# Linear attention into a two-layer token network: the order of the last two token tiles, and the last 128 tokens in two pieces

## The chip, the cores and the metric

The kernel runs on one core of one Trainium2 chip. The core has a matrix engine (TensorE, "PE" in the profile, with "PEld" for its weight loads), VectorE ("DVE"), ScalarE ("ACT"), GpSimd ("POOL") and SyncE ("SP"), which here only issues DMA transfers. Each engine runs its own list of instructions in order and waits on semaphores for the others; a DMA is issued by an engine's queue and carried out by 16 DMA engines. Matmuls write to PSUM, whose banks hold 512 float32 columns of 128 partitions each; everything else lives in SBUF. The metric is the device time of one execution in microseconds; lower is better.

## The reference

```python
def _attn_ref(q, k, v):                    # 8 blocks x 8 heads x 576 positions x 64
    q_s = np.exp(q - np.max(q, axis=-1, keepdims=True))
    q_s = q_s / (np.sum(q_s, axis=-1, keepdims=True) + 1e-09)
    k_s = np.exp(k - np.max(k, axis=2, keepdims=True))
    k_s = k_s / (np.sum(k_s, axis=2, keepdims=True) + 1e-09)
    kv = np.einsum('bhsd,bhse->bhde', k_s, v)
    return np.einsum('bhsd,bhde->bhse', q_s, kv)

def _moe_ref(x, w_in, w_out):              # x: 4608 x 512, w_in: 512 x 2048, w_out: 2048 x 512
    h = x @ w_in
    g = np.maximum(0.01 * h, h)
    return g @ w_out
```

The attention's output, with its heads side by side, is `x`. Inputs and output are float32.

## The kernel before

**Tiles.** The 4608 tokens are nine tiles of 512 (`TT`), numbered 0 to 8; the attention has eight blocks `b` of 576 tokens, so block 7 covers tokens 4032 to 4607: the last 64 of tile 7 and all of tile 8. `xT` holds the attention's output in bf16, features on partitions. For tiles 1 to 6 the loop at L916 does layer 1 as 16 groups `j` of four matmuls (`layer1`, L564), each into a PSUM bank `ph` that ScalarE turns into half of a tile `gj` with a leaky ReLU (`leaky`, L573); then layer 2 as four groups `tsub` of 128 tokens and 16 matmuls each (`layer2`, L585) into a bank `pout`, copied to `out_sb` and stored by two DMAs of 64 rows (`store`, L577 to L582). `layer2_at` (L907) is a generator that yields after each matmul.

**Banks.** `psB` has six PSUM banks for nearly everything, `psO` two for `pout`. `out_sb` has four buffers, `gj` ten, the raw inputs six.

**Attention between the groups.** `at(t, u, ...)` hangs work on a place: `u` from 0 to 15 is after layer-1 group `u` of tile `t`, 16 to 31 after each quarter of its layer-2 groups. For a block these are: loads; `k_front` and `k_exp` (softmax over positions); `q_front` (maximum, L244, and subtraction, L303), `q_exp` (L311), `q_back` (sum, L320; reciprocal; normalization, L327; and `q_turn`, a transposing DMA by SyncE, L552); `attend_kv` (L505), which multiplies keys and values of the next block (`kv_quads`, L340) and queries with them (`cross`, L478), and `kd_make` (L360, L361). `x_keep` (L501 on ScalarE, L503 on VectorE) copies the result from `po` banks into `xT`. For the last block `attend_all` (L535) does queries alone, at place (6, 19), after tile 6's first layer-2 group; its 16 matmuls use six banks.

**The last two tiles as a pair.** Layer 1 of tiles 7 (`TA`, tokens `XA`) and 8 (`TB`, tokens `XB`) is one 2 x 2 block product (the two tiles by the two halves of the features `CL`, `CR`; these by the two halves of the hidden units), done with seven products in place of eight. `weight_sums` (L791, at place (6, 12)) makes the four combinations of weights `t1` to `t4` in VectorE (four subtractions of 2048 columns, L789) and a copy `b22` on GpSimd; `token_sums` (L801, at (6, 22)) makes `s1` to `s4` on VectorE (L810, L789) and `a22` on ScalarE (L813), all float32 for the matmuls. `pair_layer1(i, between)` (L951) does *block row* `i` of eight: seven `product`s of two matmuls each (L948), in this order: the first one from `xT` and `w_in` as they are, `p6` (`t2` by `s2`), `p2` (`xT` and `w_in`), `t3` by `s3`, `p5` (`t1` by `s1`), `t4` by `a22`, `b22` by `s4`. ScalarE copies the first to `e1` (L967), VectorE adds the others up in seven additions (`add`, L960), and ScalarE applies the leaky ReLU to four results: two for tile 7 (`g7`, in `gj` tiles; the fourth one of a row is held until the next row has begun, `held_leaky`), two for tile 8 (`g8`, in columns of `xT` whose tiles are done). After each product the generator `between_products` (L987) issues a *filler*, one layer-2 matmul (two after the seventh): in rows 0 and 1 tile 6's last group, from row 2 on the pair's own layer 2 for tile 7, `pair_layer2` (L937), four matmuls each on the activations of row `n - 2`. Its four banks are the two of `psO` and two of `psB`, so from row 2 on four banks are left for products. After the rows come the last 16 of these matmuls, four copies by VectorE and stores; then layer 2 of tile 8, four groups (L1018), each copied by ScalarE and stored.

Of the kernel before, what the change touches and what calls it, by code (L numbers as in the profile page):

```python
# [26 lines left out]
def kernel(  # L27
# [737 lines left out]
    for t in range(3, B - 1):  # L765
        b = t + 1
        q_front(b, t - 1, 29)
        at(t, 2, lambda b=b: q_exp(b, ALLR))
        if b + 1 < B:
            k_front(b + 1, t, 1, 8)  # L770
            casts(b + 1, t, 6)
            at(t, 17, lambda b=b: k_exp(b + 1, ALLH))
            at(t, 23, lambda b=b: attend_kv(b))
        q_back(b, t, 5)
        if b + 2 < B:
            at(t, 5, lambda b=b: load_all(b + 2))
# [38 lines left out]

    at(6, 12, weight_sums)
    at(6, 19, lambda: attend_all(B - 1, (R7,), (RE,)))
    at(6, 22, token_sums)

# [86 lines left out]

    def layer2_at(t, g, tsub, po):  # L907
        for j in range(NF):
            layer2(po, g, tsub, j)
            if j == NF - 1:  # L910
                store(t * TT + tsub * P, po, nc.scalar.copy)
            if j % 4 == 3:
                run(t, 16 + 4 * tsub + j // 4)
            yield

    for t in range(1, TA):  # L916
        g_sb = []
        for j in range(NF):
            ph = psB_pool.tile([P, TT], FP32, name="ph", tag=BANK_TAG)
            layer1(j, ph, t * TT, TT)  # L920
            if j % 2 == 0:
                g_sb.append(g_pool.tile([P, 2, TT], BF16, name="gj"))
            leaky(g_sb[j // 2][:, j % 2], ph)
            run(t, j)
        for tsub in range(NTS):
            po = psO_pool.tile([P, O], FP32, name="pout", tag="pout")
            fill = layer2_at(t, g_sb, tsub, po)
            if (t, tsub) != (TA - 1, NTS - 1):
                for _ in fill:
                    pass  # L930


    g7 = {}
    g8 = lambda j: xT[:, j % NB, j // NB * TT : (j // NB + 1) * TT]

    def pair_layer2(tsub, po, j):
        nc.tensor.matmul(  # L937
            po,
            lhsT=g7[j][:, tsub * P : (tsub + 1) * P],
            rhs=w_out_sb[:, j],  # L940
            start=(j == 0),
            stop=(j == NF - 1),
        )

    def product(i, w, a):
# [3 lines left out]
        return ps  # L949

    def pair_layer1(i, between):  # L951
        of = lambda n: (lambda c: late[n][:, c])
        wl = lambda c0: (lambda c: w_in_sb[:, c0 + c])
        xl = lambda c0: (lambda c: xT[:, c0 + c, XA])
        e1, u2, u3, u4, c22 = (late["pool"].tile([P, TT], FP32, name=n) for n in ("e1", "u2", "u3", "u4", "c22"))
        pair = g_pool.tile([P, 2, TT], BF16, name="gj")
        g7[i], g7[NH + i] = pair[:, 0], pair[:, 1]

# [7 lines left out]

        nc.scalar.copy(out=e1, in_=do(wl(0), xl(0)))  # L967
        for fn in held_leaky:
            fn()
        p6 = do(of("t2"), of("s2"))  # L970
        p2 = do(wl(2), xl(2))
        add(u2, p6, e1)
        add(e1, p2, e1)
        leaky(g7[i], e1)
        add(u3, do(of("t3"), of("s3")), u2)
        p5 = do(of("t1"), of("s1"))
        add(u4, p5, u2)
        add(c22, p5, u3)
        leaky(g8(NH + i), c22)
# [4 lines left out]

    pouts, held_leaky = [], []

    def between_products():  # L987
        for n in range(NH):
            if n < 2:
                todo = [lambda: next(fill, None)] * 8  # L990
            else:
                if n == 2:
                    pouts.extend(psO_pool.tile([P, O], FP32, name="pout", tag="pout") for _ in range(2))
                    pouts.extend(psB_pool.tile([P, O], FP32, name="pout2", tag=BANK_TAG) for _ in range(2))
                todo = [
                    lambda tsub=tsub, j=j: pair_layer2(tsub, pouts[tsub], j)
                    for j in (n - 2, NH + n - 2)
                    for tsub in range(NTS)
                ]
            for k in range(7):  # L1000
                for fn in todo[k : k + 1 + k // 6]:
                    fn()
                yield

    between = between_products()
    for i in range(NH):
        pair_layer1(i, between)
    held_leaky[0]()
    for i in range(NH - 2, NH):
        for j in (i, NH + i):  # L1010
            for tsub in range(NTS):
                pair_layer2(tsub, pouts[tsub], j)
    for tsub in range(NTS):
        store(TA * TT + tsub * P, pouts[tsub])
    for tsub in range(NTS):
        po = psB_pool.tile([P, O], FP32, name="pout2", tag=BANK_TAG)
        for j in range(NF):
            nc.tensor.matmul(  # L1018
                po,
                lhsT=g8(j)[:, tsub * P : (tsub + 1) * P],  # L1020
                rhs=w_out_sb[:, j],
                start=(j == 0),
                stop=(j == NF - 1),
            )
        store(TB * TT + tsub * P, po, nc.scalar.copy)
    assert not hooks, list(hooks)
# [30 lines left out]
```

## Time and profile before

| | |
|---|---|
| time, median of 3 runs | 282.3 us (282.1 to 282.39) |
| the profiled execution | 282.17 us |
| its span in the profile | 280.4 us |
| its mean granted TensorE clock | 0.997 |
| TensorE busy | 270.9 us, 97% of the span |
| VectorE busy | 208.8 us, 74% |
| ScalarE busy | 164.4 us, 59% |
| GpSimd busy | 50.4 us, 18% |
| end of tile 6's layer 1 | 205.82 us |
| the eight block rows | 216.90 to 257.90 us |
| start of tile 8's layer 2 | 261.77 us |

The span is what the profiler saw, from the first instruction to the last event; the rest of the execution's time lies around it. In a timeline a line gives start and duration in microseconds, the engine, the line of the kernel, the operation, `out<-in` and the shape; brackets behind it give the idle time before it and what ended that. The chain of waits is followed back from the last instruction, and tells which engine set the end at each moment. A view by stretches cuts the span at given times, with each engine's busy time and number of instructions in each stretch.

### The profile page before, as it was taken

The numbers are of one execution on the slowest core, as the hardware profiler recorded it, in microseconds if no ns is written. First come the engines' busy times: TensorE is split into PE (matmuls) and PEld (weight loads), VectorE is DVE, ScalarE is ACT, GpSimd is POOL, SyncE is SP. The second block draws the span as 40 slices with busy tenths as digits, with TensorE's granted clock in tenths as the row PEclk, the third lists the DMA queues.
The fourth block names the chain that finished last, engine by engine and source line by source line (L and its number), as shares of the span: only waits on it lengthen the run. The fifth ranks groups of instructions, "written<-read, shape, count | busy, mean of one in ns | idle before, by whom it ended". The sixth has DMA issues, their size and how long they took to land.

```text
span 280.4 us, 4875 instructions
## 1 busy us (share of the span) xinstructions
PE 270.9 (97%) x1895; PEld 134.3 (48%) x1922; DVE 208.8 (74%) x292; ACT 164.4 (59%) x291; POOL 50.4 (18%) x56
## 2 busy tenths in 40 slices
PE   8899999999999999999999999999999989999993
PEld 3488644444444554445444444444444545544441
DVE  3986986999999959948793779452898788888400
ACT  4977483782597368744775467644845555655220
POOL 2957460358003004000400050100000000000000
PEclk9999999999999999999999999999999999999998
DMA  7999999986992697099219830333033110000273
GB/s 254 327 207 325 250 233 310 394 292 177 351 408 87 101 385 258 8 320 353 65 32 315 315 79 2 84 77 75 1 87 75 37 37 2 0 1 0 65 162 75
DMA packets 39847, 46.46 MB, mean 166 GB/s; under 512 B 18704, under 2 KB 23056, under 8 KB 39824
## 3 DMA queue, kind: packets, MB, share of 16 engines
q1 hardware_dynamic: 36320, 41.95, 47.8%
q0 software_dynamic: 3504, 4.20, 8.6%
q8 instruction: 15, 0.25, 0.3%
q14 instruction: 8, 0.07, 0.1%
HBM read 36.70 MB, written 9.44 MB: 165 GB/s over the span
## 4 chain that ended last, share of the span: by engine, by line
PE 83%; DVE 9%; ACT 2%; issue 2%; DMA 2%; SPq 0%; DVEq 0%
PE pout L585 35%; PE ph L564 34%; PE pout L1018 5%; DVE u L960 4%; PE pp L948 4%; DMA k_raw<-in_k_dram 2%; PE po L478 2%; PE pout L937 1%; DVE e L960 1%; DVE c L960 1%; DVE t L159 1%; PE pokv L340 1%; ACT e L967 1%; PE pkv L340 1%; PE pkv L418 0%
## 5 line engine op out<-in xcount | busy, mean ns | idle before, releaser
L585 PE MATMUL pout<-w_out_sb,gj 128*128 128x512 bf16 x432 | 100.6, 379 | 1.1 <-issue 0.3
L564 PE MATMUL ph<-xT,w_in_sb 128*128 128x512 bf16 (+1 forms) x505 | 98.3, 352 | 0.4
L573 ACT ACTIVATE gj<-ph 128x512 bf16<-128x512 f32 x112 | 63.2, 603 | 17.6 <-PE ph L564 16.7
L564 PEld LDWEIGHTS <-w_in_sb 128*128 128x128 bf16 x512 | 49.8, 98 | 47.0 <-DMA w_in_sb<-in_moe_w_in_dram 0.3
L585 PEld LDWEIGHTS <-gj 128*128 128x128 bf16 x448 | 42.8, 98 | 52.4 <-issue 2.9
L579 ACT COPY out_sb<-pout 128x512 f32<-128x512 f32 x28 | 16.3, 583 | 52.7 <-PE pout L585 19.4
L217 POOL CAST vb<-v_raw 128x1152 bf16<-128x1152 f32 x13 | 20.1, 1577 | 83.7 <-DMA v_raw<-in_v_dram 67.8
L320 DVE TENSOR_REDUCE qsum<-qe 128x36 f32<-128x2304 bf16 (+5 forms) x13 | 20.1, 1542 | 10.5 <-ACT qe L311 10.3
L205 ACT ACTIVATE ke<-k_raw 128x2304 bf16<-128x2304 f32 (+2 forms) x13 | 18.0, 1386 | 9.4 <-DVE k_raw L197 9.0
L327 DVE TENSOR_TENSOR qe<-qe,qrec 128x2304 bf16<-128x2304 bf16 (+5 forms) x13 | 21.5, 1657 | 0.4
L960 DVE TENSOR_TENSOR u<-pp,u 128x512 f32<-128x512 f32 x32 | 20.6, 684 | 0.8
L937 PE MATMUL pout<-w_out_sb,gj 128*128 128x512 bf16 x62 | 20.4, 384 | 0.7 <-ACT out_sb L579 0.6
L244 DVE TENSOR_REDUCE qmax<-q_raw 128x36 f32<-128x2304 f32 (+5 forms) x13 | 20.0, 1540 | 0.3 <-DMA q_raw<-in_q_dram 0.3
L311 ACT ACTIVATE qe<-q_raw 128x2304 bf16<-128x2304 f32 (+5 forms) x13 | 17.1, 1317 | 4.4 <-POOL q_raw L303 3.5
L197 DVE TENSOR_TENSOR k_raw<-k_raw,kall 128x1152 f32<-128x1152 f32 (+2 forms) x10 | 18.1, 1821 | 0.3
L948 PE MATMUL pp<-s,t 128*128 128x512 f32 x48 | 18.2, 479 | 0.0
L360 DVE RECIPROCAL krec<-pokv 128x2 f32<-128x2 f32 x8 | 1.3, 165 | 20.4 <-PE pokv L478 20.4
L303 POOL TENSOR_TENSOR q_raw<-q_raw,qmax 128x512 f32<-128x512 f32 (+3 forms) x7 | 11.8, 1682 | 20.7 <-DVE qmax L244 20.2
L501 ACT CAST xT<-po 128x448 bf16<-128x448 f32 (+3 forms) x34 | 14.4, 516 | 1.1 <-PE po L478 1.1
L159 DVE TENSOR_TENSOR t<-t 128x256 f32<-128x256 f32 (+2 forms) x22 | 14.0, 637 | 0.7
L1018 PE MATMUL pout<-w_out_sb,xT 128*128 128x512 bf16 x62 | 13.9, 379 | 0.1
L303 DVE TENSOR_TENSOR q_raw<-q_raw,qmax 128x2304 f32<-128x2304 f32 (+1 forms) x6 | 13.2, 2202 | 0.2
(97 smaller groups left out, 247.5 us busy)
## 6 DMA issues: line engine op xcount, KB each, us to landing
out_dram<-out_sb SPq DMA_DIRECT2D x72, 128.0 KB, 3.0
q_raw<-in_q_dram SPq DMA_DIRECT2D x6, 1152.0 KB, 9.2
v_raw<-in_v_dram SPq DMA_DIRECT2D x6, 1152.0 KB, 11.9
k_raw<-in_k_dram SPq DMA_DIRECT2D x5, 1152.0 KB, 6.6
k_raw<-in_k_dram SPq DMA_DIRECT2D x6, 576.0 KB, 6.1
v_raw<-in_v_dram SPq DMA_DIRECT2D x4, 576.0 KB, 7.5
w_in_sb<-in_moe_w_in_dram POOLq DMA_DIRECT2D x7, 256.0 KB, 7.1
w_out_sb<-in_moe_w_out_dram POOLq DMA_DIRECT2D x6, 256.0 KB, 9.5
```

Of the source, the lines that this page charges most:

```text
L217: eng.tensor_copy(out=o, in_=i)
L244: nc.vector.tensor_reduce(out=o, in_=st[b]["q"][:, hs, rs], axis=AX.X, op=ALU.max)
L303: eng.tensor_tensor(out=qs, in0=qs, in1=st[b]["qmax", rs.start, hs.start].unsqueeze(3).to_broadcast([P, m, n, D]), op=ALU.subtract,)
L320: nc.vector.reduce_sum(out=qsum, in_=q_cols(b, rs, hs), axis=AX.X)
L327: nc.vector.tensor_tensor(out=qes if out is None else out, in0=qes, in1=st[b]["qrec", rs.start, hs.start].unsqueeze(3).to_broadcast([P, n, ...
L564: nc.tensor.matmul(ph, lhsT=w_in_sb[:, cb, j * P : (j + 1) * P], rhs=xT[:, cb, c0 : c0 + n], start=(cb == 0 and first), stop=(cb == NB - 1 ...
L573: nc.scalar.activation(out=o, in_=ph, func=AF.Prelu, alpha=LEAKY_SLOPE)
L585: nc.tensor.matmul(pout, lhsT=g_sb[j // 2][:, j % 2, tsub * P : (tsub + 1) * P], rhs=w_out_sb[:, j, os], start=(j == 0), stop=(j == NF - 1),)
L937: nc.tensor.matmul(po, lhsT=g7[j][:, tsub * P : (tsub + 1) * P], rhs=w_out_sb[:, j], start=(j == 0), stop=(j == NF - 1),)
L948: nc.tensor.matmul(ps, lhsT=w(c)[:, i * P : (i + 1) * P], rhs=a(c), start=(c == 0), stop=(c == 1))
L960: nc.vector.tensor_tensor(out=o, in0=ps, in1=e, op=ALU.add)
L1018: nc.tensor.matmul(po, lhsT=g8(j)[:, tsub * P : (tsub + 1) * P], rhs=w_out_sb[:, j], start=(j == 0), stop=(j == NF - 1),)
```

## The change

*Block 7's queries* (hunk 1): `q_front(7)` goes to (5, 19), `q_exp(7)` to (5, 24), `q_back(7)` to (5, 25); before, these stood at (5, 29), (6, 2) and (6, 5). *The head of the pair* (hunk 2): `weight_sums` goes to (6, 2); the last `attend_all` and `token_sums` to (6, 15), that is between tile 6's two layers, with `x_keep` shared out to ScalarE and VectorE. *Tile 6's layer 2*: only its first group comes ahead of the pair; the other three are the fillers of rows 0 to 5. *First products*: `pair_first(i + 1)` issues the first product of a row and its copy to `e1` in row `i`, between `p5` and `t4`. `g7` of rows 2 to 7 goes to columns of `xT` that are done. *The pair's layer 2*: in row 6 `pair_step` does four matmuls each for groups 2 and 3 (banks of `psB`), in row 7 four each for groups 0 and 1 (banks of `psO`); 48 more follow the rows. *Tile 8's layer 2*: the first three groups are copied by VectorE; the last one is done as 384 and then 128 columns, copied by ScalarE and VectorE, with one of the two DMAs of each issued by ScalarE.

```diff
@@ -763,15 +763,15 @@
     at(2, 22, lambda: k_exp(4, H0), lambda: k_exp(4, H1))
     at(2, 27, lambda: attend_kv(3))
     for t in range(3, B - 1):
-        b = t + 1
-        q_front(b, t - 1, 29)
-        at(t, 2, lambda b=b: q_exp(b, ALLR))
-        if b + 1 < B:
+        b, last = t + 1, t + 2 == B
+        q_front(b, t - 1, 19 if last else 29)
+        at(t - last, 24 if last else 2, lambda b=b: q_exp(b, ALLR))
+        if not last:
             k_front(b + 1, t, 1, 8)
             casts(b + 1, t, 6)
             at(t, 17, lambda b=b: k_exp(b + 1, ALLH))
             at(t, 23, lambda b=b: attend_kv(b))
-        q_back(b, t, 5)
+        q_back(b, t - last, 25 if last else 5)
         if b + 2 < B:
             at(t, 5, lambda b=b: load_all(b + 2))
 
@@ -813,9 +813,8 @@
         nc.scalar.copy(out=late["a22"], in_=xT[:, CR, XB])
         subtract(nc.vector, "s4", xT[:, CR, XA], plain("s2"))
 
-    at(6, 12, weight_sums)
-    at(6, 19, lambda: attend_all(B - 1, (R7,), (RE,)))
-    at(6, 22, token_sums)
+    at(6, 2, weight_sums)
+    at(6, 15, lambda: attend_all(B - 1, (R7, (nc.scalar, nc.vector)), (RE, (nc.scalar, nc.vector))), token_sums)
 
     def g_tiles():
         return [g_pool.tile([P, 2, TT], BF16, name="gj") for _ in range(NF // 2)]
@@ -904,7 +903,8 @@
     for tsub in range(NTS):
         store(tsub * P, pout[tsub])
 
-    def layer2_at(t, g, tsub, po):
+    def layer2_at(t, g, tsub):
+        po = psO_pool.tile([P, O], FP32, name="pout", tag="pout")
         for j in range(NF):
             layer2(po, g, tsub, j)
             if j == NF - 1:
@@ -922,25 +922,14 @@
                 g_sb.append(g_pool.tile([P, 2, TT], BF16, name="gj"))
             leaky(g_sb[j // 2][:, j % 2], ph)
             run(t, j)
-        for tsub in range(NTS):
-            po = psO_pool.tile([P, O], FP32, name="pout", tag="pout")
-            fill = layer2_at(t, g_sb, tsub, po)
-            if (t, tsub) != (TA - 1, NTS - 1):
-                for _ in fill:
-                    pass
+        for tsub in range(NTS if t < TA - 1 else 1):
+            for _ in layer2_at(t, g_sb, tsub):
+                pass
 
 
     g7 = {}
-    g8 = lambda j: xT[:, j % NB, j // NB * TT : (j // NB + 1) * TT]
-
-    def pair_layer2(tsub, po, j):
-        nc.tensor.matmul(
-            po,
-            lhsT=g7[j][:, tsub * P : (tsub + 1) * P],
-            rhs=w_out_sb[:, j],
-            start=(j == 0),
-            stop=(j == NF - 1),
-        )
+    spent = lambda n: xT[:, n % NB, n // NB * TT : (n // NB + 1) * TT]
+    g8 = spent
 
     def product(i, w, a):
         ps = psB_pool.tile([P, TT], FP32, name="pp", tag=BANK_TAG)
@@ -948,13 +937,22 @@
             nc.tensor.matmul(ps, lhsT=w(c)[:, i * P : (i + 1) * P], rhs=a(c), start=(c == 0), stop=(c == 1))
         return ps
 
+    of = lambda n: (lambda c: late[n][:, c])
+    firsts, held_leaky = {}, []
+
+    def pair_first(i):
+        firsts[i] = e1 = late["pool"].tile([P, TT], FP32, name="e1")
+        ps = product(i, lambda c: w_in_sb[:, c], lambda c: xT[:, c, XA])
+        nc.scalar.copy(out=e1, in_=ps)
+
     def pair_layer1(i, between):
-        of = lambda n: (lambda c: late[n][:, c])
-        wl = lambda c0: (lambda c: w_in_sb[:, c0 + c])
-        xl = lambda c0: (lambda c: xT[:, c0 + c, XA])
-        e1, u2, u3, u4, c22 = (late["pool"].tile([P, TT], FP32, name=n) for n in ("e1", "u2", "u3", "u4", "c22"))
-        pair = g_pool.tile([P, 2, TT], BF16, name="gj")
-        g7[i], g7[NH + i] = pair[:, 0], pair[:, 1]
+        e1 = firsts[i]
+        u2, u3, u4, c22 = (late["pool"].tile([P, TT], FP32, name=n) for n in ("u2", "u3", "u4", "c22"))
+        if i < 2:
+            pair = g_pool.tile([P, 2, TT], BF16, name="gj")
+            g7[i], g7[NH + i] = pair[:, 0], pair[:, 1]
+        else:
+            g7[i], g7[NH + i] = (spent(NF + 2 * (i - 2) + n) for n in range(2))
 
         def add(o, ps, e):
             nc.vector.tensor_tensor(out=o, in0=ps, in1=e, op=ALU.add)
@@ -964,17 +962,17 @@
             next(between)
             return ps
 
-        nc.scalar.copy(out=e1, in_=do(wl(0), xl(0)))
+        add(u2, do(of("t2"), of("s2")), e1)
         for fn in held_leaky:
             fn()
-        p6 = do(of("t2"), of("s2"))
-        p2 = do(wl(2), xl(2))
-        add(u2, p6, e1)
-        add(e1, p2, e1)
+        add(e1, do(lambda c: w_in_sb[:, 2 + c], lambda c: xT[:, 2 + c, XA]), e1)
         leaky(g7[i], e1)
         add(u3, do(of("t3"), of("s3")), u2)
         p5 = do(of("t1"), of("s1"))
         add(u4, p5, u2)
+        if i + 1 < NH:
+            pair_first(i + 1)
+            next(between)
         add(c22, p5, u3)
         leaky(g8(NH + i), c22)
         add(u3, do(of("t4"), of("a22")), u3)
@@ -982,47 +980,67 @@
         add(u4, do(of("b22"), of("s4")), u4)
         held_leaky[:] = [lambda: leaky(g7[NH + i], u4)]
 
-    pouts, held_leaky = [], []
+    pouts, started = {}, [0] * NTS
+    turn = [j for i in range(NH) for j in (i, NH + i)]
+
+    def pair_step(tsub):
+        j = turn[started[tsub]]
+        started[tsub] += 1
+        if tsub not in pouts:
+            pool, tag = (psO_pool, "pout") if tsub < 2 else (psB_pool, BANK_TAG)
+            pouts[tsub] = pool.tile([P, O], FP32, name="pout", tag=tag)
+        nc.tensor.matmul(
+            pouts[tsub],
+            lhsT=g7[j][:, tsub * P : (tsub + 1) * P],
+            rhs=w_out_sb[:, j],
+            start=(started[tsub] == 1),
+            stop=(started[tsub] == NF),
+        )
+
+    def fill_steps():
+        for tsub in range(1, NTS):
+            yield from layer2_at(TA - 1, g_sb, tsub)
+        for tsubs in ((2, 3), (0, 1)):
+            for _ in range(4):
+                for tsub in tsubs:
+                    pair_step(tsub)
+                    yield
 
     def between_products():
+        fill = fill_steps()
         for n in range(NH):
-            if n < 2:
-                todo = [lambda: next(fill, None)] * 8
-            else:
-                if n == 2:
-                    pouts.extend(psO_pool.tile([P, O], FP32, name="pout", tag="pout") for _ in range(2))
-                    pouts.extend(psB_pool.tile([P, O], FP32, name="pout2", tag=BANK_TAG) for _ in range(2))
-                todo = [
-                    lambda tsub=tsub, j=j: pair_layer2(tsub, pouts[tsub], j)
-                    for j in (n - 2, NH + n - 2)
-                    for tsub in range(NTS)
-                ]
             for k in range(7):
-                for fn in todo[k : k + 1 + k // 6]:
-                    fn()
+                for _ in range(1 + k // 6):
+                    next(fill)
                 yield
 
     between = between_products()
+    pair_first(0)
+    next(between)
     for i in range(NH):
         pair_layer1(i, between)
     held_leaky[0]()
-    for i in range(NH - 2, NH):
-        for j in (i, NH + i):
-            for tsub in range(NTS):
-                pair_layer2(tsub, pouts[tsub], j)
+    next(between, None)
+    while started[0] < NF:
+        for tsub in range(NTS):
+            pair_step(tsub)
     for tsub in range(NTS):
         store(TA * TT + tsub * P, pouts[tsub])
     for tsub in range(NTS):
-        po = psB_pool.tile([P, O], FP32, name="pout2", tag=BANK_TAG)
-        for j in range(NF):
-            nc.tensor.matmul(
-                po,
-                lhsT=g8(j)[:, tsub * P : (tsub + 1) * P],
-                rhs=w_out_sb[:, j],
-                start=(j == 0),
-                stop=(j == NF - 1),
-            )
-        store(TB * TT + tsub * P, po, nc.scalar.copy)
+        row0 = TB * TT + tsub * P
+        last = tsub == NTS - 1
+        pieces = ((slice(0, 384), nc.scalar.copy), (slice(384, O), nc.vector.tensor_copy))
+        for os, copy in pieces if last else ((slice(0, O), nc.vector.tensor_copy),):
+            po = psB_pool.tile([P, os.stop - os.start], FP32, name="pout2", tag=BANK_TAG)
+            for j in range(NF):
+                nc.tensor.matmul(
+                    po,
+                    lhsT=g8(j)[:, tsub * P : (tsub + 1) * P],
+                    rhs=w_out_sb[:, j, os],
+                    start=(j == 0),
+                    stop=(j == NF - 1),
+                )
+            store(row0, po, copy, os, (nc.sync, nc.scalar) if last else (nc.sync, nc.sync))
     assert not hooks, list(hooks)
```

## The prediction

> **What bounds the kernel now.** I read the page's first two parts, then the chain of waits, then stretches cut at the borders of the last stages, then the timelines of TensorE, VectorE and ScalarE there, and last the stores at the end.
>
> ```profile
> span 280.4 us, 4875 instructions
> PE 270.9 (97%) x1895; PEld 134.3 (48%) x1922; DVE 208.8 (74%) x292; ACT 164.4 (59%) x291; POOL 50.4 (18%) x56
> PE 83%; DVE 9%; ACT 2%; issue 2%; DMA 2%; SPq 0%; DVEq 0%
> ...
> 205.82 1.08 PE pout L585 x5
> 209.28 0.61 PE po L478 x16
> 209.89 5.07 PE pout L585 x23
> ```
>
> TensorE sets the end nearly everywhere; only its gaps and what follows its last matmul can be won. From the end of tile 6's first layer (205.82) one layer-2 group of 16 matmuls takes 209.28 - 205.82 = 3.46 us, the last attention 0.61. DVE's 9% of the chain lies in the paired rows, so those are cut out next, one row to a stretch (columns: length, busy time of PE, PEld, DVE, ACT, POOL, clock, DMA):
>
> ```profile
> 216.90:221.88 4.98, 4.98 (x24) 2.67 (x22) 3.71 (x7) 2.16 (x4) 0.00 (x0) 1.00 0.23 53
> ...
> 226.86:232.62 5.76, 5.12 (x24) 2.74 (x22) 4.49 (x8) 3.41 (x7) 0.00 (x0) 1.00 0.20 46
> ...
> 252.80:257.90 5.10, 5.10 (x23) 2.42 (x21) 4.32 (x7) 2.90 (x5) 0.00 (x0) 1.00 0.00 0
> ```
>
> In the timeline of TensorE stands what stopped row 2, and in the chain how the rows end:
>
> ```profile
> 228.62 0.38 PE L937 MATMUL pout<-w_out_sb,gj 128*128 128x512 bf16 x1 [0.64 <-ACT out_sb L579]
> 260.73 1.04 PE pout L937 x4
> 261.77 0.22 PE pout L1018
> 272.83 2.77 PE pout L1018 x12
> ```
>
> Row 0 runs at 4.98 us, busy throughout: TensorE's own pace for 7 products and 8 layer-2 matmuls. Row 2 takes 5.76: its first matmul into a `pout` bank of its own waits 0.64 us for ScalarE to empty tile 6's. The eight rows end at 257.90, so they take 41.00 us where 8 x 4.98 = 39.84 would do: 1.16 lost. (PE looks full in the last row, at 5.10, because a matmul that waits for its operands counts as busy.) The 16 matmuls from 257.90 to 261.77 take 3.87 against 3.46: 0.41 more, spent on the last activation of row 7. Together 1.57 us.
>
> The timelines of VectorE and ScalarE over one of the late rows:
>
> ```profile
> 239.59 0.69 DVE L960 TENSOR_TENSOR u<-pp,e 128x512 f32<-128x512 f32 x1 [0.57 <-ACT e L967]
> ...
> 242.97 1.29 DVE L960 TENSOR_TENSOR u<-pp,u 128x512 f32<-128x512 f32 x2
> 244.84 0.69 DVE L960 TENSOR_TENSOR u<-pp,e 128x512 f32<-128x512 f32 x1 [0.57 <-ACT e L967]
> ...
> 243.70 0.63 ACT L573 ACTIVATE xT<-u 128x512 bf16<-128x512 f32 x1 [0.16 <-DVE u L960]
> 244.24 0.57 ACT L967 COPY e<-pp 128x512 f32<-128x512 f32 x1
> ```
>
> This is the loop of the late rows. VectorE's seven additions run from 239.59 to 242.97 + 1.29 = 244.26; then it idles for 0.57 us until ScalarE has copied the next row's first product (244.24 to 244.81), which stands behind an activation in ScalarE's order. Period: 244.84 - 239.59 = 5.25 us, against TensorE's 4.98. Without the idle time VectorE needs some 4.67 a row.
>
> **The change, part by part.** *First product ahead.* It takes its bank and its copy into `e1` before the last three additions of the row before. The copy then waits only for its product and for the activation of `e1`, both done by mid row. VectorE's period falls to 4.67 and TensorE's 4.98 leads; 0.31 us a row is there to catch up. The number of products and fillers stays 56 and 64.
>
> *Tile 6's layer 2 as filler.* Three of its groups (48 matmuls) move into rows 0 to 5; rows 6 and 7 start the pair's layer 2 on activations of rows 0 and 1, long done; the other 48 follow the rows. The 0.64 us goes, since no `pout` bank is wanted just after a group's end, and the last activation is wanted some 40 matmuls (9 us) after row 7, so the 0.41 goes. In rows 0 to 5 all six banks serve products. In rows 6 and 7 four do, as before in rows 2 to 7; counted from the order of releases, with products 0.71 us apart (4.98 / 7), the tightest bank is free about a microsecond ahead if VectorE keeps up.
>
> *Attention ahead.* It now starts at 205.82 instead of 209.28, and its last two banks are those of tile 6's last two activations. The rows of ScalarE, VectorE, GpSimd and SyncE, in the timelines:
>
> ```profile
> 205.86 0.60 ACT L573 ACTIVATE gj<-ph 128x512 bf16<-128x512 f32 x1 [0.20 <-PE ph L564]
> 209.84 2.40 ACT L501 CAST xT<-po 128x448 bf16<-128x448 f32 x6
> 212.28 1.23 DVE L810 TENSOR_TENSOR s<-xT 128x1024 fp32r<-128x1024 bf16 x1 [0.51 <-ACT xT L501]
> 215.81 1.22 DVE L789 TENSOR_TENSOR s<-xT,s 128x1024 fp32r<-128x1024 bf16 x1
> ...
> 176.13 2.56 DVE L197 TENSOR_TENSOR k_raw<-k_raw,kall 128x2304 f32<-128x2304 f32 x1
> 185.05 0.17 DVE L360 RECIPROCAL krec<-pokv 128x2 f32<-128x2 f32 x1 [6.36 <-PE pokv L478]
> 185.86 2.54 DVE L244 TENSOR_REDUCE qmax<-q_raw 128x36 f32<-128x2304 f32 x1
> 197.28 2.55 DVE L320 TENSOR_REDUCE qsum<-qe 128x36 f32<-128x2304 bf16 x1 [6.28 <-ACT qe L311]
> ...
> 186.07 0.70 ACT L501 CAST xT<-pokv 128x256 bf16<-128x256 f32 x2
> 195.13 2.12 ACT L311 ACTIVATE qe<-q_raw 128x2304 bf16<-128x2304 f32 x1
> 202.99 1.91 SPq L552 DMA_TRANSPOSE qX<-qe  x1
> 161.37 3.80 POOL L217 CAST vb<-v_raw 128x1152 bf16<-128x1152 f32 x2 [24.49 <-DMA v_raw<-in_v_dram]
> ```
>
> The last activation ends at 206.46, where the first three quarters of the attention would be through at about 206.2: a wait of 0.3 us (0 if ScalarE is early, 0.6 if it is a whole activation late). That is the price of this part, unless its followers come too late. Its matmuls end at 206.73. Six evacuations, now three each on ScalarE and VectorE, took 2.40 on one engine, so some 1.2 to 1.6: done at 207.9. Then the four sums at 1.18 pitch (212.28 to 215.81 for three): `s2` at 210.3, `s4` at 212.6. TensorE does tile 6's first group from 206.73 to 210.19, one first product and one filler, and wants `s2` at 210.85: half a microsecond to spare. VectorE begins adding at 212.6, about 0.9 late, caught up in three rows at 0.31, and with six banks nothing waits for it.
>
> The softmax of block 7 must move ahead for this. VectorE is idle from 178.69 (176.13 + 2.56) for 6.36 us; `qmax` and subtraction are 5.1, so they end at 183.8, ahead of the reciprocal at 185.05 that is queued behind them. The exponential (2.12) follows ScalarE's evacuations, which end at 186.77, and makes one store copy some 0.3 late, whose bank nobody wants before 205. The row sum then starts at 188.9 where it started at 197.28, so it and what follows on VectorE without a gap, weight sums included, is over 8.4 us sooner. Before, that stretch ran up to the 0.51 us of idle time ahead of 212.28, to 211.77; now it ends at 203.4, and VectorE is next wanted at 206.2. The queue of SyncE carries the transposing DMA now ahead of four stores of tile 5: the norm ends near 194.4 and the transposing issue takes 1.91, so they wait till about 196.4, and their buffers are wanted again after tile 6's stores begin at 210. Was `q` there at 178.69? `v` of the same block, behind it in the same queue, was cast at 161.37.
>
> *Last 128 tokens in two pieces.* First the timeline of TensorE for narrow matmuls, then groups of narrow copies, then the end in the timeline and in stretches:
>
> ```profile
> 20.56 0.39 PE L444 MATMUL psum_qt<-ident,qe 128*128 128x128 bf16 x4
> 20.79 0.27 PE L564 MATMUL ph<-xT,w_in_sb 128*128 128x256 bf16 x1
> 21.87 8.91 PE L564 MATMUL ph<-xT,w_in_sb 128*128 128x256 bf16 x80
> ```
>
> ```profile
> L361 DVE TENSOR_TENSOR kd<-pokv,krec 128x128 bf16<-128x128 f32 x8 | 2.3, 292 | 0.3
> L501 ACT CAST xT<-po 128x384 bf16<-128x384 f32 x6 | 2.5, 497 | 0.0
> ```
>
> ```profile
> 275.62 0.59 ACT L579 COPY out_sb<-pout 128x512 f32<-128x512 f32 x1 [2.87 <-PE pout L1018]
> 276.23 1.10 SPq L582 DMA_DIRECT2D out_dram<-out_sb  x2
> ```
>
> ```profile
> 277.00:277.40 0.40, 0.00 (x0) 0.00 (x0) 0.00 (x0) 0.00 (x0) 0.00 (x0) 1.00 0.15 36
> 277.40:278.00 0.60, 0.00 (x0) 0.00 (x0) 0.00 (x0) 0.00 (x0) 0.00 (x0) 1.00 0.84 195
> 278.70:280.37 1.67, 0.00 (x0) 0.00 (x0) 0.00 (x0) 0.00 (x0) 0.00 (x0) 0.50 0.00 0
> ```
>
> Now: matmuls end at 275.60 (272.83 + 2.77), the copy at 276.21, two issues take 1.10, data flows from 277.33 (36 GB/s in that slice is 0.07 us of the flow after it) to 278.70, and 1.67 us close the span. So data ends 3.10 us after the last matmul.
>
> After: four 128-column matmuls took 0.23 us from start to start, 0.0575 each; 80 of 256 columns took 8.75, 0.109 each; 384 lies between 0.109 and 0.216 at 0.1625. So 16 x 0.1625 + 16 x 0.0575 = 3.52 us against 3.46. By the Trainium skill, "TensorE: Matmul & The Clock Gate", section Back-to-back issue gap, a stream of weight load and matmul pairs holds only about 81 ns at 128 columns, which would make the small piece 1.30 us, and the end 0.38 later than I sum; the row above says 58, though for transposes.
>
> Call the last matmul's end E. The 384 piece is ready at E - 0.92; its copy is 0.50, its data starts 1.10 after issue, at E + 0.73, and 192 KB at 195 to 203 GB/s end at E + 1.7. The small copy is at most 0.29, its issues go out on two queues at E + 0.35, its data could start at E + 1.45 but queues behind the large piece until E + 1.7; 64 KB more end at E + 2.03. Gain 3.10 - 2.03 = 1.07. No row shows a store issued by ScalarE or one of 512-byte rows. At best the small data does not queue, a gain of 1.3. At worst each small packet costs what one of 2 KB does: both pieces then take 1.3 us of transfer each and end at E + 3.3, a loss of 0.2. I take 1.07, since the issue is of the same kind as SyncE's.
>
> **The sum.** 206.73 + 3.46 + 39.84 + 48 x 0.216 (10.38) + three groups (10.37) + 3.52 = 274.30, 1.30 before 275.60. With the tail: -2.37 us. The profiled execution took 282.17 in all; 279.8. The runs' median is 282.3, 0.13 above it: 279.9.
>
> **The rivals.** *The tail gives nothing.* For it: the unknown queue and packets. Against: the copy alone is shorter by 0.3. Then only 1.30 is won and up to 0.2 lost: 281.0 to 281.2.
>
> *The rows stay at VectorE's pace, so the change does not do what it says.* If VectorE cannot do better than 5.25, the rows take 42.0 from 210.19, TensorE ends at 276.4, 0.8 later, and the tail gives most back: 282.0. For it: seven additions of 0.684 are 4.79 with no gap, close to 4.98. Against: they overlap, as the loop's 4.67 shows.
>
> *The head comes late, slower.* Place: VectorE ahead of the first product that needs `s2`. Had `q` of block 7 not landed by 178.69 and `qmax` run at 185.86 as before, weight sums, evacuations and token sums come 7.2 us later. Slack is 2.8 (203.4 to 206.2) and 0.55 (210.3 to 210.85), so TensorE stands still for 3.85 us: 279.9 + 3.85 = 283.8. It decides against the change once VectorE is more than 3.35 + 2.4 = 5.75 us late. Against it: the cast at 161.37.
>
> **How the numbers follow.** Forecast 0.78 (within 279.4 to 280.9), no gain in the tail 0.11, rows at VectorE's pace 0.07, late head 0.04. Range: best 282.3 - 1.57 (no wait at the attention) - 1.3 = 279.4; worst with dense rows 282.3 - 0.97 + 0.2 = 281.5. I put 279.3 to 281.5. About 0.2%, 0.56 us, is what a measurement of this kernel tells from no change: faster 0.88, same 0.07, slower 0.05.
>
> **What would show it.** Right: eight rows near 4.98 with no PE gap, no idle time of VectorE put down to ScalarE's `e` copy except in row 0, the last matmul near 274.3, data ending about 2 us behind it. Wrong: rows of 5.2; a PE gap over 0.5 at the first `s2` product, or in rows 6 and 7 for a bank; the 128-column stretch above 1.3 us; ScalarE's issues over 1 us, or the span ending more than 4.2 us after the last matmul.

## The result and the profile after

| | before | after |
|---|---|---|
| time, median of 4 runs each | 282.35 us (282.10 to 282.43) | 280.43 us (280.27 to 280.48) |
| ratio, 95% interval | | 0.9933 (0.9915 to 0.995) |
| the profiled execution, and its span | 282.17, 280.4 us | 280.43, 278.6 us |
| end of tile 6's layer 1 | 205.82 us | 206.31 us |
| start of tile 8's layer 2 | 261.77 us | 261.15 us |
| last matmul's end | 275.60 us | 275.02 us |
| from there to the span's end | 4.8 us | 3.6 us |

The kernel is 1.92 us faster by the medians, where 2.4 was forecast; 280.43 lies inside the range. The page of after, first its span and engines, then the shares of its chain of waits:

```profile
span 278.6 us, 4917 instructions
PE 270.6 (97%) x1912; PEld 135.7 (49%) x1938; DVE 213.0 (76%) x299; ACT 162.5 (58%) x285; POOL 51.7 (19%) x56
...
PE 92%; DVE 3%; DMA 2%; issue 1%; ACT 0%; SPq 0%
```

VectorE's share of the chain went from 9% to 3%: the rows no longer run at its pace. The same stretches as before, now at the borders of after's rows 0, 2 and 6 and of the 48 matmuls behind the rows:

```profile
210.90:215.88 4.98, 4.98 (x24) 2.75 (x22) 4.89 (x7) 2.16 (x4) 0.00 (x0) 1.00 0.24 56
...
220.86:225.85 4.99, 4.99 (x23) 2.67 (x22) 4.74 (x8) 3.78 (x7) 0.00 (x0) 1.00 0.23 53
...
240.80:245.80 5.00, 4.95 (x22) 2.67 (x22) 4.79 (x8) 3.56 (x7) 0.00 (x0) 1.00 0.23 54
...
250.63:261.00 10.37, 10.32 (x49) 4.67 (x49) 1.53 (x3) 1.57 (x3) 0.00 (x0) 1.00 0.00 0
```

Row 2 fell from 5.76 to 4.99 us, a late row from 5.10 to 5.00 (VectorE's period there from 5.25 to 5.00); the 48 matmuls behind the rows take 10.37. The head of the stage, in the chain of waits and then in VectorE's timeline:

```profile
206.34 0.61 ACT gj L573
...
206.99 0.30 PE po L478 x6
207.28 0.16 issue
207.44 3.40 PE pout L585 x15
```

```profile
209.54 1.22 DVE L789 TENSOR_TENSOR s<-s,xT 128x1024 fp32r<-128x1024 f32 x1
...
212.96 0.68 DVE L958 TENSOR_TENSOR u<-pp,e 128x512 f32<-128x512 f32 x1
...
231.28 0.69 DVE L958 TENSOR_TENSOR u<-pp,u 128x512 f32<-128x512 f32 x1 [0.15 <-PE pp L937]
```

The attention is the chain's one weak place. Its last six matmuls wait for tile 6's last activation and end at 207.28. The 0.16 us behind them, put down to issue, is in all likelihood no wait but a matmul whose record is missing: a group of layer 2 has 16 matmuls, this one's 16 weight loads are recorded, and the row shows 15 matmuls. A run described below changes only who issues the last DMAs, so its head is the same. Its chain has the whole group, without a gap:

```profile
207.07 3.56 PE pout L585 x16
```

That is 0.16 + 3.40. So layer 2 starts at 207.28, 0.97 us after layer 1's end at 206.31, where 0.61 + 0.3 was summed. `s2` is ready at 210.76 and the additions start at 212.96. Once VectorE has caught up, its only idle time within the rows is of the kind in the last row: twice 0.15 us and once 0.46, for TensorE.

The end, in the timelines of TensorE's followers and then the issues of the large piece's two transfers (KB of each, median us from issue to landing):

```profile
274.19 0.48 ACT L579 COPY out_sb<-pout 128x384 f32<-128x384 f32 x1 [21.82 <-PE pout L1036]
274.70 1.39 ACTq L582 DMA_DIRECT2D out_dram<-out_sb  x2
275.04 0.29 DVE L579 COPY out_sb<-pout 128x128 f32<-128x128 f32 x1 [2.80 <-PE pout L1036]
```

```profile
out_dram<-out_sb SPq DMA_DIRECT2D x1, 96.0 KB, 2.1
out_dram<-out_sb ACTq DMA_DIRECT2D x1, 96.0 KB, 2.4
```

The large piece's copy starts at 274.19, the small piece's at 275.04: the 16 matmuls of 128 columns between them take 0.85 us, 53 ns each. The span cut into slices there:

```profile
275.40:275.80 0.40, 0.00 (x0) 0.00 (x0) 0.00 (x0) 0.00 (x0) 0.00 (x0) 1.00 0.00 0
275.80:276.20 0.40, 0.00 (x0) 0.00 (x0) 0.00 (x0) 0.00 (x0) 0.00 (x0) 1.00 0.84 196
...
276.60:277.00 0.40, 0.00 (x0) 0.00 (x0) 0.00 (x0) 0.00 (x0) 0.00 (x0) 1.00 0.61 167
277.00:277.40 0.40, 0.00 (x0) 0.00 (x0) 0.00 (x0) 0.00 (x0) 0.00 (x0) 1.00 0.01 3
```

Data flows from 275.8 to 277.0, which is E + 1.98 with E = 275.02 (before: E + 3.10).

### The profile page after: what moved, and what is told of

Read it like the earlier page. It is cut to its first block, busy times and chain, and to the rows that moved or that the text cites. A ratio compares the mean times of both kernels' runs of the same rounds, so it can differ in the third digit from the quotient of the medians.

```text
span 278.6 us, 4917 instructions
## 1 busy us (share of the span) xinstructions
PE 270.6 (97%) x1912; PEld 135.7 (49%) x1938; DVE 213.0 (76%) x299; ACT 162.5 (58%) x285; POOL 51.7 (19%) x56
## 4 chain that ended last, share of the span: by engine, by line
PE 92%; DVE 3%; DMA 2%; issue 1%; ACT 0%; SPq 0%
PE pout L585 35%; PE ph L564 35%; PE pp L937 9%; PE pout L992 5%; PE pout L1036 5%; DMA k_raw<-in_k_dram 2%; PE po L478 1%; DVE t L159 1%; PE pokv L340 1%; PE pkv L340 1%; PE pkv L418 0%; DVE k_raw L409 0%; DVE e L958 0%; ACT ke L205 0%; DVE kmax L159 0%
## 5 line engine op out<-in xcount | busy, mean ns | idle before, releaser
L585 PE MATMUL pout<-w_out_sb,gj 128*128 128x512 bf16 x432 | 104.7, 380 | 1.1 <-issue 0.5
L579 ACT COPY out_sb<-pout 128x512 f32<-128x512 f32 (+1 forms) x25 | 14.5, 579 | 56.2 <-PE pout L1036 21.8
L217 POOL CAST vb<-v_raw 128x1152 bf16<-128x1152 f32 x13 | 21.4, 1680 | 82.7 <-DMA v_raw<-in_v_dram 82.7
L579 DVE COPY out_sb<-pout 128x512 f32<-128x512 f32 (+1 forms) x12 | 7.3, 652 | 18.8 <-PE pout L992 8.8
L303 DVE TENSOR_TENSOR q_raw<-q_raw,qmax 128x2304 f32<-128x2304 f32 (+1 forms) x6 | 14.7, 2448 | 0.2
L1036 PE MATMUL pout<-w_out_sb,xT 128*128 128x512 bf16 (+2 forms) x79 | 14.0, 336 | 0.1
L501 ACT CAST xT<-po 128x448 bf16<-128x448 f32 (+3 forms) x31 | 13.3, 513 | 1.1 <-PE po L478 1.1
```

Of the source, the lines that this page charges most:

```text
L217: eng.tensor_copy(out=o, in_=i)
L303: eng.tensor_tensor(out=qs, in0=qs, in1=st[b]["qmax", rs.start, hs.start].unsqueeze(3).to_broadcast([P, m, n, D]), op=ALU.subtract,)
L579: copy(out=out_sb, in_=pout)
L585: nc.tensor.matmul(pout, lhsT=g_sb[j // 2][:, j % 2, tsub * P : (tsub + 1) * P], rhs=w_out_sb[:, j, os], start=(j == 0), stop=(j == NF - 1),)
L1036: nc.tensor.matmul(po, lhsT=g8(j)[:, tsub * P : (tsub + 1) * P], rhs=w_out_sb[:, j, os], start=(j == 0), stop=(j == NF - 1),)
```

## The experiments

Each run is compared with runs of the kernel before on the same chip; "stage" is the time from the end of tile 6's layer 1 to the last matmul in the run's profile: 69.78 us before, 68.71 after, 68.48 by the forecast (274.30 - 205.82).

**Two parts of the change, alone.** The kernel before with only the first product of each row issued in the row ahead. Attention and query work stay where they were. The fillers keep their order, one behind each product; with a product more ahead of it, each comes one product earlier in its row:

```diff
-        nc.scalar.copy(out=e1, in_=do(wl(0), xl(0)))
-        for fn in held_leaky:
-            fn()
         p6 = do(of("t2"), of("s2"))
-        p2 = do(wl(2), xl(2))
         add(u2, p6, e1)
-        add(e1, p2, e1)
+        for fn in held_leaky:
+            fn()
+        add(e1, do(wl(2), xl(2)), e1)
...
         add(u4, p5, u2)
+        if i + 1 < NH:
+            pair_first(i + 1, between)
         add(c22, p5, u3)
```

> The kernel before with one part of the change: each row's first product and its copy in the row ahead, fillers and all else as before. My theory: rows 3 to 7 fall to 4.98 us and the wait for the last activation shrinks, 0.9 us together, while row 2 keeps its 0.64 us wait for the pout bank: 281.4 us. Rival, that the order of products is not what holds the rows: 282.3 us.

Measured: 280.84 us against 282.26, 0.9948 (0.9935 to 0.996). That is 1.42 us won, 0.5 more than the theory gave it, because the wait in row 2 went too. Row 2 in stretches, and then, from the chain, the 18 layer-2 matmuls that end the rows:

```profile
227.04:232.03 4.99, 4.99 (x23) 2.67 (x23) 4.55 (x8) 3.48 (x7) 0.00 (x0) 1.00 0.23 53
```

```profile
256.59 3.90 PE pout L937 x18
```

No gap in row 2, and 3.90 / 18 = 0.217 us a matmul at the end: no wait for the last activation either. ScalarE's timeline shows the copy of tile 6's last bank, here and then in the kernel before:

```profile
227.16 0.57 ACT L579 COPY out_sb<-pout 128x512 f32<-128x512 f32 x1
227.63 0.63 ACT L573 ACTIVATE xT<-u 128x512 bf16<-128x512 f32 x1
```

```profile
227.47 0.63 ACT L573 ACTIVATE xT<-u 128x512 bf16<-128x512 f32 x1 [0.16 <-DVE u L960]
228.01 0.57 ACT L579 COPY out_sb<-pout 128x512 f32<-128x512 f32 x1
```

The copy runs 0.85 us sooner although row 2 begins 0.18 later (227.04 against 226.86). The two rows of each view show why: the copy has changed places with an activation. It is issued with tile 6's last filler, and since that filler comes one product earlier in its row, the copy now stands ahead of the activation of `u` in ScalarE's order, and no longer behind it and its wait for VectorE. The activation ahead of both starts at 226.62 here and at 226.67 in the kernel before; with the 0.54 that lie between its start and the copy's here, the copy could have started at about 227.21 there (an estimate). So 0.80 of the 0.85 is the place in the order, and 0.05 is what ran late. The bank is now empty at 227.73, and its filler runs at 228.20.

The kernel before with only the last 128 tokens in two pieces, VectorE's copies for tile 8 and the second queue:

```diff
-        po = psB_pool.tile([P, O], FP32, name="pout2", tag=BANK_TAG)
-        for j in range(NF):
...
-        store(TB * TT + tsub * P, po, nc.scalar.copy)
+        pieces = ((slice(0, 384), nc.scalar.copy), (slice(384, O), nc.vector.tensor_copy))
+        for os, copy in pieces if last else ((slice(0, O), nc.vector.tensor_copy),):
...
+            store(row0, po, copy, os, (nc.sync, nc.scalar) if last else (nc.sync, nc.sync))
```

> The kernel before with one part of the change: tile 8's copies by VectorE and its last 128 tokens as 384 and 128 columns, one DMA of each piece issued by ScalarE. My theory: the tail alone is worth 1.1 us (data ends 2.0 us after the last matmul instead of 3.1), so 281.2 us; rows and head as before. Rival, that the gain in the tail comes from elsewhere: 282.3 us. On the start of the execution: if the .5 us later first load in the changed kernel's profile belongs to the second issuing queue, VectorE's first instruction starts near 5.1 us here too and the gain is only 0.6 us; if it is scatter between executions, it starts anywhere between 4.5 and 5.2 us.

Measured: 281.32 us, 0.9964 (0.9951 to 0.9978), 0.94 won. The tail works by itself; the rival by which it gives nothing falls.

Both parts together, without the moves of attention, query work and fillers (the two diffs above):

> The kernel before with two parts of the change: first product ahead and the last 128 tokens in two pieces; attention, query work and fillers as before. My theory: the two parts add up (0.94 and 1.42 us alone), so 279.9 us, which is no slower than the whole change: the moves of attention and fillers bring nothing and cost the wait ahead of the attention. Rival, that the moves are needed for dense rows or a dense end: 280.4 us or more, with PE idle in rows 2 to 7 or ahead of tile 8.

Measured: 279.79 us against 282.44, 0.9905 (0.9891 to 0.9919): 0.64 under the changed kernel's 280.43. The end of its chain:

```profile
256.80 3.90 PE pout L937 x18
260.97 13.60 PE pout L1032 x78
274.59 0.29 DVE out_sb L579
```

Its stage is 68.35 us (206.22 to 274.57) where the changed kernel's is 68.71. The run with the first product alone has 68.30. The moves thus bring nothing that the first product ahead has not brought already, and cost some 0.36 us of stage. That is what the attention takes more in the changed kernel: 0.97 us against 0.61, as in the kernel before. The rest of the 0.64 lies outside the stage, and the two ratios' intervals still touch (0.9919 and 0.9915).

**One part undone.** The changed kernel with each first product back at the head of its own row:

```diff
     def pair_layer1(i, between):
+        pair_first(i)
+        next(between)
         e1 = firsts[i]
...
-        if i + 1 < NH:
-            pair_first(i + 1)
-            next(between)
...
```

> The changed kernel with each row's first product issued at the head of its own row again. My theory: VectorE goes back to a period of 5.25 us with 0.57 us of idle time a row behind ScalarE's copy; it runs later and later behind TensorE, nothing waits in rows 0 to 5 with six banks, and in rows 6 and 7 with four banks TensorE waits 1.3 to 1.7 us in all: 281.7 to 282.1 us. Rival, that the new order of the fillers alone makes the rows dense: 280.4 us.

Measured: 283.57 us, 1.0045 (1.0033 to 1.0058): slower than the kernel before, and 3.1 us over the changed one, about twice what was expected. VectorE's timeline, at the first additions of two rows:

```profile
217.62 0.69 DVE L960 TENSOR_TENSOR u<-pp,e 128x512 f32<-128x512 f32 x1 [0.57 <-ACT e L946]
...
223.35 0.69 DVE L960 TENSOR_TENSOR u<-pp,e 128x512 f32<-128x512 f32 x1 [1.06 <-ACT e L946]
```

The wait for the `e1` copy is back, and 0.5 longer in every other row. ScalarE's timeline ahead of the second of them shows why:

```profile
222.26 0.57 ACT L579 COPY out_sb<-pout 128x512 f32<-128x512 f32 x1
222.73 0.59 ACT L946 COPY e<-pp 128x512 f32<-128x512 f32 x1
```

A `pout` bank of tile 6 falls due every second row, and its copy stands ahead of the `e1` copy. VectorE's periods are so 5.25 and 5.73 us, by turns. TensorE keeps its 5.00 a row at first, living on free banks, and pays later, in rows 5 and 6:

```profile
235.40:240.90 5.50, 5.35 (x24) 2.55 (x23) 4.72 (x8) 2.90 (x5) 0.00 (x0) 1.00 0.14 34
240.90:248.30 7.40, 6.04 (x24) 2.59 (x23) 5.76 (x11) 4.01 (x7) 0.00 (x0) 1.00 0.15 37
```

The changed kernel with all four last DMAs issued by SyncE:

```diff
-            store(row0, po, copy, os, (nc.sync, nc.scalar) if last else (nc.sync, nc.sync))
+            store(row0, po, copy, os)
```

> The changed kernel with all four DMAs of the last two pieces issued by SyncE. My theory: the second queue saves SyncE's issue time only; SyncE is still issuing for the large piece when the small one is ready, so data ends 0.3 to 0.6 us later: 280.7 to 281.0 us. Rival, that opening a second queue costs 0.5 us at the start of the execution: VectorE's first instruction goes back from 5.1 to 4.6 us and the time stays at 280.4 or below.

Measured: 280.97 us, 0.9952 (0.9939 to 0.9964). The second queue is worth 0.54 us by the medians. The two ratios' intervals overlap, but the runs' times do not (280.86 to 281.03 against 280.27 to 280.48), and in the profiles the span ends 4.4 us behind the last matmul here and 3.6 in the changed kernel. The queue costs nothing at the start: VectorE's first instruction here comes at 4.92 us, and at 5.11 (changed kernel) and 4.62 (first product in its row) with it.

The changed kernel with block 7's query work and the weight sums at their old places, which makes the late head of the third rival:

```diff
-        q_front(b, t - 1, 19 if last else 29)
-        at(t - last, 24 if last else 2, lambda b=b: q_exp(b, ALLR))
+        q_front(b, t - 1, 29)
+        at(t, 2, lambda b=b: q_exp(b, ALLR))
...
-        q_back(b, t - last, 25 if last else 5)
+        q_back(b, t, 5)
...
-    at(6, 2, weight_sums)
+    at(6, 12, weight_sums)
```

> The changed kernel with block 7's query work and the weight sums back at their old places, the attention still ahead of tile 6's second layer. This tries the price of the rival with a late head. My theory: VectorE ends the weight sums 8 us later than in the changed kernel, its slack is some 3 us, and TensorE stands still for 4 to 5 us, at the attention's followers or at the first s2 product: 284.2 to 285.3 us. Rival, that VectorE has more slack than counted: under 283 us.

Measured: 287.2 us, 1.0171 (1.0155 to 1.0186), more than either theory gave. TensorE's timeline, and then the stretches around its longest gap:

```profile
207.27 0.68 PE L478 MATMUL po<-qX,kd 64*64 64x448 bf16 x16 [1.14 <-DMA qX<-qe]
...
212.66 0.38 PE L937 MATMUL pp<-xT,w_in_sb 128*128 128x512 bf16 x1 [0.93 <-DVE xT L503]
...
216.21 0.82 PE L937 MATMUL pp<-s,t 128*128 128x512 f32 x2 [2.95 <-DVE s L789]
```

```profile
214.00:216.00 2.00, 0.00 (x0) 0.00 (x0) 1.97 (x3) 1.57 (x3) 0.00 (x0) 1.00 0.00 0
216.00:218.00 2.00, 1.79 (x5) 0.77 (x6) 2.00 (x3) 0.00 (x0) 0.00 (x0) 0.66 0.60 139
218.00:220.00 2.00, 2.00 (x6) 1.17 (x5) 1.91 (x4) 0.25 (x1) 0.00 (x0) 0.50 0.00 0
220.00:222.00 2.00, 2.00 (x11) 0.96 (x10) 1.63 (x3) 1.03 (x3) 0.00 (x0) 0.99 0.00 0
```

The first product with `s2` comes at 216.21, against 211.14 in the changed kernel. Three waits come to 5.02 us: 1.14 for the transposed queries, 0.93 and 2.95 for VectorE. Then something that no theory had: after the long gap the granted clock is 0.50, and 6 matmuls fit into 2 us where 11 follow at 0.99.

**A repair.** If the attention waits for the last activation, then its second half can come a quarter of a layer-2 group later:

```diff
-    at(6, 15, lambda: attend_all(B - 1, (R7, (nc.scalar, nc.vector)), (RE, (nc.scalar, nc.vector))), token_sums)
+    at(6, 15, lambda: attend_all(B - 1, (R7, (nc.scalar, nc.vector))))
+    at(6, 16, lambda: attend_all(B - 1, (RE, (nc.scalar, nc.vector))), token_sums)
```

> The changed kernel with the last two positions of the last attention (the two banks that wait for tile 6's last activations) one quarter of a layer-2 group later. My theory: the 0.5 us that TensorE loses between tile 6's first layer and its first layer-2 group goes (206.30 to 207.44 becomes the 0.61 us of the matmuls), and s2 comes 0.1 to 0.2 us later, just in time: 279.9 us. Rival, that the token sums are then late and TensorE waits as long at the first s2 product: 280.4 us.

Measured: 280.13 us, 0.9918 (0.9905 to 0.9931). The time is 0.3 lower, but the stage is 68.71 us as before the repair: this profile's layer 1 merely ended earlier, at 206.01. Its chain:

```profile
206.01 0.50 PE po L478 x8
206.51 0.16 issue
206.67 0.81 PE pout L585 x3
207.48 0.24 PE po L478 x8
207.72 2.70 PE pout L585 x12
...
211.06 0.60 PE pp L938 x2
```

Attention and waits now take 0.50 + 0.24 = 0.74 us, 0.23 less than the 0.97. The 0.16 is again the place of a missing record: four layer-2 matmuls are issued between the halves, and three are shown. But these four take 0.16 + 0.81 = 0.97 where four at 0.217 would take 0.87. With the 2.70 of the other twelve the group comes to 3.67, 0.11 more than the 3.56 in one piece. And the first `s2` product takes 0.60 in place of some 0.47: VectorE has the last columns later, `s2` is ready at 210.82 (4.81 behind layer 1's end, against 4.45), and TensorE meets it. 0.11 + 0.13 give back what 0.23 won. So the stage gains nothing; a gain from this order is not borne out.

**The same kernels again**, to see how far the start scatters.

> The changed kernel once more, for the start of the execution alone. If the time at which the first load lands belongs to the program, VectorE starts at 5.1 us again; if it is scatter between executions, it starts anywhere from 4.6 to 5.2 us, as the six profiles so far (4.59 to 5.22 us, with the second issuing queue at 5.11, 5.22 and 4.62, without it at 4.59, 4.92 and 4.80).

> The kernel before once more, for the start of the execution alone. In its first profile VectorE started at 4.59 us and tile 6's first layer ended at 205.82, the earliest of all ten profiles so far; the changed kernel's two stand at 5.11 and 4.99, 206.31 and 206.13. If the start belongs to the program, it is 4.6 and 205.8 again, and 0.3 to 0.5 us of the change's expected gain was lost there; if it is scatter between executions, the start falls anywhere from 4.6 to 5.2 us.

Measured: 280.24 and 282.43 us. VectorE's first instruction waits for the first load. It comes at 4.59 us in the first profile of the kernel before, and at 4.99 in the second:

```profile
4.59 1.28 DVE L253 TENSOR_REDUCE nmax<-q_raw 128x8 f32<-128x512 f32 x2 [4.59 <-DMA q_raw<-in_q_dram]
```

```profile
4.99 1.28 DVE L253 TENSOR_REDUCE nmax<-q_raw 128x8 f32<-128x512 f32 x2 [4.99 <-DMA q_raw<-in_q_dram]
```

Layer 1 ends at 205.82 and 206.10 there, and at 206.31 and 206.13 in the two of the changed kernel. The stages differ by 0.03 us at most between two profiles of one kernel (69.78 and 69.75; 68.71 and 68.70), so it is the start that scatters.

## Why the prediction was right, and where it was not

**The sum, term by term.** From 210.84, the end of the first group of tile 6's layer 2, to the last matmul the profile has 64.18 us; the forecast had 64.11 (210.19 to 274.30). So row, filler and small-piece terms are confirmed together. The difference of the two profiled times, 280.43 against 279.8, is made of others: layer 1 ended 0.49 later, the attention cost 0.97 instead of 0.91 us, the group behind it 3.56 instead of 3.46, and the span ended 3.58 behind the last matmul, 1.19 less than before where the gain was put at 1.07. 0.49 + 0.06 + 0.10 + 0.07 - 0.12 = 0.60 of the 0.63.

**Right: the wait in the attention. Mis-sized: the group behind it.** The "wait of 0.3 us" had the right mechanism and nearly the size: 0.97 - 0.61 = 0.36. The group behind the attention was summed at 3.46, the size of a group that follows layer 1. The kernel before shows the difference already: behind its attention 32 matmuls take 7.01 us (209.89 to 216.90), 0.09 more than twice 3.46. Why it is so stays open.

**The base.** The sum was built on the border at 205.82, of the execution with the earliest start of the two. The 0.13 by which that execution lay under the median was added; the repeats show that this was less than the scatter of the start, 0.4 between two profiles of one kernel.

**Right: first product ahead.** With it alone the late rows reach 4.99, without it the changed kernel is slower than the one before.

**Wrong: what the fillers are for.** "The 0.64 us goes, since no `pout` bank is wanted just after a group's end, and the last activation is wanted some 40 matmuls (9 us) after row 7, so the 0.41 goes." Both went with the fillers of the kernel before. The 0.41 had the cause of the late rows: in the chain of the kernel before, VectorE's loop leads up to the last activation and to the matmuls that wait for it at 260.73:

```profile
258.72 0.70 DVE u L960
...
260.07 0.61 ACT gj L573
```

The 0.64 had another: the copy of tile 6's bank stood behind an activation in ScalarE's order. With the first product ahead it stands in front of that activation, which nobody had planned; that this one edit won both was luck. No run tried the copy's place alone. The prediction gave these two waits a cure of their own, the moves of fillers and attention, that was not needed; the total, 1.57, came out about right all the same (1.47 in the run with the first product alone: 260.49 - 206.01 = 54.48 against 55.95). The wait in the attention, whose move made tile 6's groups free as fillers, is what holds the changed kernel above that.

**Right: the head.** Weight sums were forecast to end at 203.4 and ended at 203.79, `s2` at 210.3 and was ready at 210.76, 0.38 ahead of its product at 211.14 where 0.55 was forecast. What was moved into tiles 5 and 6 cost TensorE nothing there: from VectorE's first instruction to the end of layer 1 it is 201.23 us before (4.59 to 205.82) and 201.20 after (5.11 to 206.31).

**Right: the tail.** E + 2.03 was forecast, E + 1.98 measured, and alone it won 0.94. The rate of 81 ns at 128 columns, which the Trainium skill gives ("TensorE: Matmul & The Clock Gate", section Back-to-back issue gap), is not borne out here: 53 ns, and 0.85 us for the piece instead of 1.30.

**The rivals.** The tail that gives nothing falls with the tail-only run. Rows at VectorE's pace were priced at 282.0; where they do occur, with the first product in its own row, the kernel takes 283.57. The price assumed a steady 5.25 and left out that the store copies, now ahead of `e1` in every other row, make the wait 1.06. The late head was priced at 283.8 and costs 287.2. VectorE is 8.3 us late here and not 7.2 (its weight sums end at 212.07 against 203.79), for which the prediction's rule, with 3.35 us of slack, gives 284.8. It left out the transposing DMA, which is late as well (1.14), and the clock. TensorE's timeline of the changed kernel, and of the late one, from the first `s2` product to the second plain one behind it:

```profile
211.14 0.82 PE L937 MATMUL pp<-s,t 128*128 128x512 f32 x2
...
214.07 0.59 PE L937 MATMUL pp<-xT,w_in_sb 128*128 128x512 bf16 x2
```

```profile
220.65 0.59 PE L937 MATMUL pp<-xT,w_in_sb 128*128 128x512 bf16 x2
```

The same work takes 2.93 us (211.14 to 214.07) and 4.44 (216.21 to 220.65): 1.5 more. With the `s2` product 5.07 later that makes 6.6, nearly the 6.77 between the medians. Both ways to lose were underrated in size; the reasons against them held.

## What to carry to other kernels

Where two engines feed each other in a loop, cure the loop first and look again: a wait elsewhere that seems to have its own cause (here the last activation, 0.41) may be the same lateness, and moving work around it can then only cost. When one instruction moves, read the new order on every engine that serves it: here a store copy and an activation changed places, and 0.64 us went with that. When a forecast is summed against one profile, take the length of the stage and not its clock time: here stages repeat to 0.03 us and starts to 0.4. When a stall of the matrix engine is priced, add what the granted clock takes after it.

## What the hardware showed that was not expected

- The granted clock fell to 0.50 after TensorE had done only about 0.6 us of work between 211.73 and 216.21 (two gaps, 0.93 and 2.95 us), and was back at 0.99 in the stretch from 220.00 (the run with the query work at its old place). The Trainium skill ("TensorE: Matmul & The Clock Gate", section What's actually happening) tells of half the clock after an idle window of about 3.4 us; here the longest full stop was shorter than that.
- The subtraction of 128 x 2304 for block 7 took 4.03 us in the changed kernel and 2.56 at its old place. GpSimd's copy `b22` (1.90 us from 181.39) runs beside it in the first and not in the second. VectorE's timeline of after:

```profile
181.66 4.03 DVE L303 TENSOR_TENSOR q_raw<-q_raw,qmax 128x2304 f32<-128x2304 f32 x1
```

  The slack there covered it (the reciprocal followed at 185.62, 0.57 later than before, of which 0.49 is the later start). The subtraction takes 1.47 longer, and the copy had 1.63 to run when it began; that the copy is the cause was not tried by itself.
- Issuing two of the last four DMAs from a second queue is worth 0.54 us, at the very end, where nothing is left to hide an issue. SyncE alone takes 2.38 us for the four, and the last issue ends 2.06 behind the last matmul (274.48 + 2.38 against 274.80); with ScalarE's two the last one ends 1.07 behind it (274.70 + 1.39 against 275.02). By the Trainium skill ("DMA: Bandwidth & Descriptors", section Issuing engines are not separate DMA queues) a second issuing engine saves the issue time alone; the traces agree, since the issues end 0.99 sooner and the span 0.8.
